# GateLoop and a SwiGLU block on one core: refitted schedule model, last output by halves, prefetch hints at the closing branch

## The chip, the cores and the metric

The kernel runs on one core of a Trainium2 chip. The engines are named as in the profile: PE is TensorE (matrix products; PEld its weight loads), DVE is VectorE, ACT is ScalarE, POOL is GpSimd, SP is SyncE, which here issues DMAs only. The metric is the time of one execution on the chip in microseconds (us): before, the median of three runs is 697.68 us (697.25 to 699.55). All numbers are float32.

## The reference

Four batches of eight heads with 768 positions of 48 features go through a linear attention with complex decay, the heads are laid side by side (384 features for each of 3072 tokens), and a SwiGLU block with RMS norm follows.

```python
mag = sqrt(a_re**2 + a_im**2);  scale = minimum(mag, 0.999) / (mag + 1e-6)
for t in range(S):                       # S = 768, per batch and head
    S_re, S_im = ar*S_re - ai*S_im + k[t] v[t]^T,  ar*S_im + ai*S_re     # 48 x 48
    y[t] = q[t] @ S_re
x = y, heads side by side                # 3072 x 384
xn = x / sqrt(mean(x*x) + 1e-6) * rms_g
out = (silu(xn @ w_gate) * (xn @ w_val)) @ w_out    # 384 -> 1536 -> 384
```

The three weight matrices arrive as float64.

## The kernel before

**Tiling.** Tokens are cut in 24 chunks of 128 (six for each batch). Gates are computed in units: chunks 0 and 1 are units of their own, the later units are pairs. Chunks also form twelve groups of two, and a group goes through the SwiGLU block together. Stages are named in the code: `load`, `kq`, `size`, `root`, `turn` and `rot` belong to the gates of a unit (magnitudes, rsqrt, angles by arctan and sin, q and k rotated by the accumulated decay), `attend`, `y`, `state` and `norm` to a chunk, `head` and `feed` to a group, `raw` and `w` to a piece of weights, `look` to a check of the weights' words.

**Gates and attention.** A unit's gates run mostly on ACT and DVE. ACT needs tables for sin, arctan, rsqrt and silu in turn, and each change is an ACT_TABLE_LOAD. The rotated q and k (`rot`, `kin`) are sent by six DMAs of SP into the tile kq, in the layout that attention needs: 96 rows (48 real and 48 imaginary) for each head. Chunks 0 to 3 alternate between kq0 and kq1; from chunk 4 on there is kq0 alone. On PE a chunk is scores (bank<-kq), masked by DVE (am<-causal,bank), then `y` (am,ve and kq,state), transposes of k (ident,kq) and the state's update (vn,kt). For the norm, ACT squares y, PE sums by a product with ones (ones,sq), ACT writes the sum to ssv, POOL raises it to the power -1/2 (rs<-ssv,mhalf), and the result is spread over the partitions: for chunks 4 to 21 by two DMAs, for the others by a PE product (ident,rs). DVE multiplies into xT.

**Weights.** Pieces of 128x3072 words come by POOL's DMA queue into space borrowed from wo and hT. ACT scales the low words (wo<-wo or hT<-hT, int32), and three DVE instructions (a shift, a bit operation and a custom addition) put the float32 weights into wg and wv. A piece's DMA waits for the piece two before it, by a small POOL copy (junk<-wo), and piece 4 for the copy seen<-kq1.

**Feed.** Group 0's first blocks (`head`) take one chunk at a time with 128-column products; the others have 256 columns. Groups from 2 on use sums of weight blocks to save products (`joint`), and `down` (L1418) gives the output product of a group from four blocks of 192 columns: x1 to x4 are PE's sums, and DVE combines them into ots[1] and ots[0]. `finish` (L1414) sends both, the last group's on ACT's DMA queue and the others on SP's.

**What sets the order.** Nothing is issued where it is written. `Flow.add` records an operation with its engine, an estimated duration and what it reads and writes; all have the helper's line 731. `dates` gives each operation a due date, backwards from the dates of the feed's products, and adds `flow.shift[(stage, i)]`. `schedule` then plays the engines forward with a model of their times: whenever an engine is free, it takes the waiting operation with the earliest due date among those that the model has ready (4.0 us are added where ACT's table would change). SP has eight lanes, so a ninth transfer waits for a landing. The order found so is what `issue` emits; each engine then works through its own queue in that order, and at run time waits for whatever is not ready.

**Fillers.** Up to WARM = 62 us of the model's time, where PE would wait, `schedule` puts in products into bank 3 of the first rotated tile with itself (bank3<-rot0). They compute nothing. They wait for the first rotated product (`started`) and keep PE busy; their number is fixed by the model, not at run time.

**End.** `fast` ends with a flag: a sum over checks of the gates and weights goes to bad. If it is above 0, `general` computes everything again in a way that has no such limits (L1675); with these inputs it is not.

Of the kernel before, what the change touches and what calls it, by code (L numbers as in the profile page):

```python
# [13 lines left out]
AF = mybir.ActivationFunctionType  # L14
ALU = mybir.AluOpType
# [4 lines left out]
C = 128  # L20
BLK = 32
# [479 lines left out]
class Flow:  # L501
# [10 lines left out]
    turn = 0.0  # L512
# [66 lines left out]
    def add(self, eng, calls, dur, reads=(), writes=(), table=None, land=None, due=None, after=(), behind=(), late=None, mode=None, group=None):  # L579
        over = self.OVERLAP.get(eng, 0.0) if land is None else 0.0  # L580
        shy = eng == "POOL" and land is None and calls[0][0] in (self.nc.gpsimd.tensor_tensor, self.nc.gpsimd.tensor_copy)
        grip = eng == "DVE" and bool(reads) and calls[0][0] != self.nc.vector.tensor_tensor_scan and not any(
            x.tensor.name in self.rooms and self.rooms[x.tensor.name][0].startswith("bank") for x in (*reads, *writes))
        op = dict(i=len(self.ops), eng=eng, calls=calls, dur=dur, deps=set(), table=table, land=land, over=over, grip=grip, shy=shy,
                  base=due, late=late, mode=mode, group=group, stage=self.stage, behind={o["i"] for o in behind})
# [30 lines left out]
    def schedule(self):  # L616
        users = self.dates()
        left = [len(op["deps"]) + len(op["behind"]) for op in self.ops]
        ready = [0.0] * len(self.ops)
        free = {}  # L620
# [12 lines left out]
        order = 0  # L633

# [8 lines left out]
        while True:  # L643
            best = None
            for eng, ops in waiting.items():
                if ops:
                    t = max(free[eng], min(ready[o["i"]] for o in ops))
                    if eng == "POOL":
                        t = min(max(free[eng], ready[o["i"]], held + 0.01 if o["shy"] else 0.0) for o in ops)
                    if eng == "SP" and len(sent) >= self.LANES:  # L650
                        if "landed" not in sent[-self.LANES]:
                            continue
                        t = max(t, sent[-self.LANES]["landed"])
                    if best is None or t < best[0]:
                        best = (t, eng)
            if queue:
                o = min(queue, key=lambda o: o["arrives"])
                t = max(served, o["arrives"])
                if best is None or t <= best[0]:
# [3 lines left out]
                    release(o, o["landed"])  # L663
                    continue
# [4 lines left out]
            for o in waiting[eng]:  # L669
                if ready[o["i"]] > t + 1e-9 or o["shy"] and t < held:  # L670
# [23 lines left out]
            if o["shy"] and t == held + 0.01:  # L694
                dur += 0.4
            if o["grip"]:
                held = t + dur
# [16 lines left out]
            order += 1  # L714
            free[eng] = t + dur - o["over"]
            release(o, t + dur, self.next)
# [17 lines left out]
def fast(tc, ctx, qT, kT, v, a_re, a_im, w_gate, w_val, w_out, rms_g, out, H, bad):  # L734
# [145 lines left out]
    def mm_time(n, m=P):  # L880
        return 2 * max(0.844e-3 * n, 0.872e-3 * m)
# [115 lines left out]
    def fetch(i, piece, raw, eng):  # L997
# [12 lines left out]
        pace = dict(load=1.9 + 1.0e-3 * raw.shape[1], lead=1.2) if eng == "POOL" else {}  # L1010
        sent = dma(raw3, src, eng, after=wait, **pace)
        if eng == "POOL":
            landed[i] = add("POOL", [(nc.gpsimd.tensor_copy, (), dict(out=junk, in_=raw[0:1, 1:2]))], 0.25,
                            after=[sent])
# [26 lines left out]
    def look(i):  # L1041
        flow.stage = "look", i
        to, ap, c, f = looks[i]
        if ap.dtype == FP32:
            for x in (small, large, whole):
                fill(x[:, i:i + 1], 0.0)
            return
        x = raws[i % len(raws)]
        lo, hi = fetch(i, looks[i], x, "SP")
        hf, lf = hi.bitcast(FP32), lo.bitcast(FP32)  # L1050
        act(hf, hf, AF.Abs, accum=whole[:, i:i + 1])
        act(lf, hf, AF.Relu, bias=most, accum=large[:, i:i + 1])
        act(lf, hf, AF.Relu, scale=-1.0, bias=least, accum=small[:, i:i + 1])
# [19 lines left out]
    def load_gates(u):  # L1073
# [15 lines left out]
        for name, ap in (("re", a_re), ("im", a_im)):  # L1089
            x = dma(t[name], ap[b].rearrange("(h j l) s -> l h j s", j=ND, l=L)[:, :, :, c * C:c * C + T],  # L1090
                    "ACT" if u < 2 and name == "im" else "SP", slow=0.75 if u > 1 else 0.0, behind=moved[HOLD] if u > 1 else (),
# [7 lines left out]
    def load_kq(u, t):  # L1099
        flow.stage = "kq", u  # L1100
        for name, ap in (("q", qT), ("k", kT)):
            for i, n in enumerate(UNITS[u]):
                dma(t[name][:, i],
                    ap[n].rearrange("d (h t) -> (d h) t", t=C).rearrange("(j p) t -> p j t", p=P),
                    behind=moved[HOLD] if u > 1 else rows_, group=("kq", u))
# [14 lines left out]
    def gates(u):  # L1120
# [85 lines left out]
        for i, n_ in enumerate(ns):  # L1206
# [4 lines left out]
            moved[n_] = [dma(kq[r:D2:2 * ND], x, "SP") for r, x in enumerate(rows[n_])]  # L1211
# [17 lines left out]
    def attend(n):  # L1229
# [5 lines left out]
        later = dict(behind=moved[min(n - 1, HOLD)] if n else (), group=("v", n))  # L1235
# [41 lines left out]
        mms(order, len(order) * mm_time(C) / 4 * 1.06, mode=BLK)  # L1277
# [36 lines left out]
        mms([(col, sq[:, j], ones, j == 0, j == parts[-1]) for j in parts], 0.25 * len(parts))  # L1314
# [103 lines left out]
    def down(ns, h, S1, S2):  # L1418
# [25 lines left out]
        tt(halves(ots[1]), halves(x1), mids[1][:, hi].unsqueeze(1).to_broadcast([C, 2, DH]), ALU.add)  # L1444
        product(x4[:, hi], S4, B[1, 1])
# [185 lines left out]
    for in_, limit, op in ((ef, P_MIN, ALU.is_ge), (ef, 1.0, ALU.is_le), (range_, 0.0, ALU.is_le),  # L1631
# [18 lines left out]
        ("attend", 11): 4.5, ("attend", 12): -1.5, ("attend", 16): 1.8, ("attend", 17): -13.3,  # L1650
        ("attend", 18): 4.0, ("attend", 19): 32.7, ("decay", 2): 6.2, ("feed", 0): 57.8, ("feed", 1): 13.4,
        ("feed", 4): 0.5, ("feed", 5): 2.1, ("feed", 6): -0.4, ("feed", 7): 57.5, ("feed", 9): 25.8,
        ("feed", 11): -11.2, ("form", 3): 17.6, ("kq", 3): -4.6, ("load", 0): 0.9, ("load", 1): -0.2,
        ("load", 2): -18.9, ("load", 3): 7.8, ("look", 10): -1.2, ("norm", 3): 0.1, ("norm", 14): 0.2,
        ("norm", 16): -2.1, ("norm", 19): 3.5, ("norm", 22): 9.5, ("raw", 0): -5.3, ("raw", 1): 3.2,
        ("root", 3): 0.2, ("root", 11): 0.2, ("rot", 2): -1.2, ("rot", 11): -19.8, ("size", 1): 1.3,
        ("size", 2): -19.9, ("size", 3): 47.2, ("size", 5): -12.4, ("size", 11): 63.2, ("state", 7): -18.0,
        ("state", 9): -18.1, ("state", 14): -10.5, ("state", 15): -17.9, ("state", 20): 19.7,
        ("state", 22): -19.0, ("turn", 1): -0.5, ("turn", 2): -0.2, ("turn", 4): -0.1, ("w", 0): 10.0,
        ("w", 1): 18.3, ("w", 2): -8.9, ("w", 3): -56.3, ("w", 5): 50.9, ("w", 7): 13.4, ("y", 6): -9.6,  # L1660
        ("y", 8): -0.5, ("y", 12): 11.1,
# [7 lines left out]
def gateloop_swiglu(tc, qT, kT, v, a_re, a_im, w_gate, w_val, w_out, rms_g, out, H):  # L1669
    nc = tc.nc  # L1670
    with tc.tile_pool(name="flag", bufs=1) as flag:
# [3 lines left out]
        with tc.If(nc.values_load(bad[0:1, 0:1]) > 0):  # L1675
            general(tc, qT, kT, v, a_re, a_im, w_gate, w_val, w_out, rms_g, out, H)

# [38 lines left out]
```

## Time and profile before

| | before |
|---|---|
| median of three runs | 697.68 us (697.25, 699.55, 697.68) |
| profiled execution | 700.69 us, 3.0 above the median |
| its span, first to last instruction | 699.0 us |
| mean granted PE clock | 0.989 |
| first product that the gates allow | 24.37 us |
| first feed product | 53.94 us |
| last product of PE | 692.09 us |
| activation table loads | 57 of 1283 ns |

The profile comes from one execution. Busy time counts instructions of an engine; the granted clock is what the throttle gave PE, 1.00 being full speed. In the timeline a row is a run of like instructions: its start, its length, engine, line, operation, output and inputs, tile shapes, and count; in brackets the engine's idle time ahead and the engine or DMA that ended it. SPq, ACTq and POOLq are the queues that issue DMAs.

### The profile page before, as it was taken

Reading aid. Unit: us, or ns where it says so; the run is one execution under the profiler, and the core shown is the slowest. Engines: PE = TensorE matmul, PEld = TensorE weight load, DVE = VectorE, ACT = ScalarE, POOL = GpSimd, SP = SyncE. Lnnn points to the kernel's source line nnn. Section 1 sums busy time; section 2 is a strip of 40 time slices with the busy share of each in tenths; the row PEclk is TensorE's granted clock in tenths of the full one; section 3 lists DMA queues with packets and bytes.
Section 4 is the critical chain, followed back from the end, with each engine's and each line's share of the span. In section 5 each row is a group of like instructions: output and inputs, shape, how many; then the busy total and the mean of one; then the engine's idle time right before and its main releaser. Section 6 shows DMA issues by size and latency. Waiting matters only on the chain.

```text
span 699.0 us, 19004 instructions
## 1 busy us (share of the span) xinstructions
PE 653.0 (93%) x7907; PEld 606.6 (87%) x7909; DVE 556.8 (80%) x1025; ACT 497.6 (71%) x864; POOL 78.9 (11%) x109
## 2 busy tenths in 40 slices
PE   0689998999999999999999999999999999999995
PEld 0679875886899999999999999999999898899995
DVE  8988979779999879879899879789889486256561
ACT  8667667896785775765878776686797765999750
POOL 3226022011013002001000002100000000000000
PEclk9979999999999999999999999999999999999999
DMA  9876671455514354253443434554140557654100
GB/s 286 284 220 205 184 214 23 114 116 121 125 28 72 80 110 75 75 111 56 112 82 70 120 71 96 139 118 110 55 88 14 135 165 186 210 187 152 54 1 28
DMA packets 104014, 82.01 MB, mean 117 GB/s; under 512 B 41936, under 2 KB 94416, under 8 KB 103920
## 3 DMA queue, kind: packets, MB, share of 16 engines
q1 hardware_dynamic: 98560, 64.78, 34.8%
q0 software_dynamic: 4416, 15.35, 10.5%
q8 instruction: 64, 1.05, 0.6%
q10 hardware_dynamic: 944, 0.59, 0.3%
q14 instruction: 30, 0.25, 0.1%
HBM read 55.84 MB, written 4.72 MB: 87 GB/s over the span
## 4 chain that ended last, share of the span: by engine, by line
PE 44%; issue 20%; DMA 10%; ACT 7%; DVE 3%; POOL 2%; SPq 1%; POOLq 0%; ACTq 0%; DVEq 0%
PE bank L731 44%; DMA sq<-rs 4%; ACT kin L731 2%; DMA hT<-in_w_out_dram 2%; POOL rs L731 2%; ACT rot L731 2%; DVE hT L731 1%; DMA row<-sq 1%; SPq L731 1%; DMA wo<-in_w_out_dram 1%; DMA rot<-in_w_val_dram 1%; ACT bank L731 1%; DMA kin<-in_w_val_dram 1%; DVE wo L731 1%; DMA kq<-kin 1%
## 5 line engine op out<-in xcount | busy, mean ns | idle before, releaser
L731 PE MATMUL bank<-wo,hT 128*128 128x192 f32 (+1 forms) x696 | 142.4, 353 | 0.6 <-DVE hT L731 0.4
L731 PEld LDWEIGHTS bank<-wo,hT 128*128 128x128 f32 x696 | 115.9, 191 | 12.2 <-issue 1.3
L731 PE MATMUL bank<-xT,wg 128*128 128x128 f32 (+1 forms) x488 | 84.8, 307 | 0.6 <-DVE wg L731 0.4
L731 ACT ACTIVATE hT<-bank 128x512 f32<-128x512 f32 x100 | 58.2, 593 | 37.7 <-PE bank L731 24.0
L731 PE MATMUL bank<-xT,wv 128*128 128x128 f32 (+1 forms) x488 | 83.5, 304 | 0.0
L731 POOL TENSOR_TENSOR rs<-ssv,mhalf 128x1 f32<-128x1 f32 x24 | 29.0, 1210 | 453.1 <-ACT ssv L731 380.4
L731 ACT ACT_TABLE_LOAD x57 | 73.1, 1283 | 7.7 <-DVE rot L731 3.9
L731 PEld LDWEIGHTS bank<-xT,wg 128*128 128x128 f32 x488 | 70.4, 191 | 6.6 <-issue 1.6
L731 PEld LDWEIGHTS bank<-xT,wv 128*128 128x128 f32 x488 | 70.9, 194 | 3.1 <-issue 0.2
L731 ACT ACTIVATE bank<-bank 128x512 f32<-128x512 f32 x60 | 35.1, 585 | 25.8 <-PE bank L731 21.2
L731 DVE TENSOR_TENSOR hT<-hT 128x768 f32<-128x768 f32 (+1 forms) x60 | 51.8, 863 | 0.4
L731 PE MATMUL bank<-yg,wg 128*128 128x128 f32 x320 | 50.6, 281 | 0.0
L731 PE MATMUL bank<-yg,wv 128*128 128x128 f32 x320 | 48.8, 275 | 0.0
L731 DVE TENSOR_TENSOR hT<-bank,hT 128x512 f32<-128x512 f32 x50 | 34.4, 688 | 15.4 <-PE bank L731 6.2
L731 DVE COPY_PREDICATED am<-causal,bank 128x512 f32<-128x512 int32 x48 | 35.0, 735 | 13.7 <-PE bank L731 13.7
L731 PE MATMUL bank<-sums,hT 128*128 128x192 f32 x240 | 45.0, 329 | 0.0
L731 PEld LDWEIGHTS bank<-yg,wg 128*128 128x128 f32 x320 | 42.1, 192 | 1.2 <-ACT sg L731 0.2
L731 ACT ACTIVATE sg<-bank 128x256 f32<-128x256 f32 (+1 forms) x72 | 38.1, 532 | 5.8 <-PE bank L731 3.9
L731 PEld LDWEIGHTS bank<-yg,wv 128*128 128x128 f32 x320 | 42.2, 192 | 0.0
L731 PE MATMUL bank<-am,ve 128*32 128x128 f32 x768 | 38.3, 281 | 1.6 <-DVE xT L731 1.4
L731 PEld LDWEIGHTS bank<-sums,hT 128*128 128x128 f32 x240 | 39.4, 190 | 0.3 <-DVE mid L731 0.2
L731 PEld LDWEIGHTS bank<-kq 96*32 96x32 f32 x1536 | 30.4, 110 | 9.8 <-issue 4.0
(217 smaller groups left out, 1449.3 us busy)
## 6 DMA issues: line engine op xcount, KB each, us to landing
kq<-rot SPq DMA_DIRECT2D x84, 128.0 KB, 2.4
kq<-kin SPq DMA_DIRECT2D x60, 128.0 KB, 2.5
kin<-in_q_dram SPq DMA_DIRECT2D x24, 192.0 KB, 3.1
kin<-in_k_dram SPq DMA_DIRECT2D x24, 192.0 KB, 3.9
out_dram<-ot SPq DMA_DIRECT2D x23, 192.0 KB, 2.5
in<-in_a_re_dram SPq DMA_DIRECT2D x11, 384.0 KB, 4.8
in<-in_a_im_dram SPq DMA_DIRECT2D x11, 384.0 KB, 4.4
vn<-in_v_dram SPq DMA_DIRECT2D x20, 192.0 KB, 2.8
```

The costliest lines, as they stand in the source:

```text
L731: fn(*args, **kw)
```

## The change

Three things change.

**The model.** `Flow.schedule` gets other durations: a PE product's end reaches other engines after 0.1 (0.055) us, a switch into the score products costs 0.225 (0.09), a table load 1.41 (1.3), PE products 0.849 and 0.877 ns an element and row (0.844, 0.872), and many DMAs get a later landing (`slow`). POOL's power is now an operation whose end is left open: if DVE works off the banks within 0.4 us of its start, it ends 0.43 us after DVE is through. A filler is counted at 0.26 us after the first ones (0.43), and fillers end when an operation writes bank 3. All dates in `flow.shift` are new. None of this is emitted: it decides only the order of the instructions and the number of fillers, which goes from 36 to 64.

**The last output.** For the last group ots[1] is sent on ACT; ots[0] is computed in halves of 192 columns, the low half earlier and sent on ACT, the high half last and sent on SP.

**The branch.** At the start PE, DVE, ACT and SP get a hint that names the closing branch, and the condition is turned round: if the flag is at most 0, the empty body is taken as the likely one; else `general` runs.

```diff
-        return 0.055 if x["eng"] == "PE" else 0.085 if x["eng"] == "POOL" else 0.034
+        return 0.1 if x["eng"] == "PE" else 0.085 if x["eng"] == "POOL" else 0.034
...
-            return 0.09
+            return 0.225 if o["stage"][0] == "attend" else 0.09
...
-        shy = eng == "POOL" and land is None and calls[0][0] in (self.nc.gpsimd.tensor_tensor, self.nc.gpsimd.tensor_copy)
+        shy = eng == "POOL" and land is None and calls[0][0] == self.nc.gpsimd.tensor_tensor
...
+            if power is not None:
+                t = held + 0.01 if shut else power["start"] + 0.4
+                if best is None or t <= best[0]:
+                    power["end"] = held + 0.43 if shut else power["start"] + power["dur"]
+                    free["POOL"] = power["end"]
...
-                dur += 1.3
+                dur += 1.41
...
-            if eng == "PE" and self.warm and t < self.warm["until"] and all("end" in x for x in self.warm["after"]):
+            if eng == "PE" and self.warm and not claimed and t < self.warm["until"] and all("end" in x for x in self.warm["after"]):
                 since = max([free["PE"]] + [x["end"] + 0.06 for x in self.warm["after"] if not recent])
-                n = int((t - since - 0.3) / 0.43)
+                step = 0.26 if recent else 0.43
+                n = int((t - since - 0.25) / step)
                 if n > 0:
                     self.fillers.append((order - 0.5, n))
-                    recent.append((since, since + 0.43 * n))
+                    recent.append((since, since + step * n))
+            claimed = claimed or o["claims"]
...
-            moved[n_] = [dma(kq[r:D2:2 * ND], x, "SP") for r, x in enumerate(rows[n_])]
+            moved[n_] = [dma(kq[r:D2:2 * ND], x, "SP", slow=0.3) for r, x in enumerate(rows[n_])]
...
+        if ns[-1] == N - 1:
+            dma(out[ns[1] * C:(ns[1] + 1) * C, :], ots[1], "ACT")
+            tt(ots[0][:, lo], mids[0][:, lo], x4[:, lo], ALU.add)
+            dma(out[ns[0] * C:(ns[0] + 1) * C, lo], ots[0][:, lo], "ACT")
+            product(x4[:, hi], S4, B[1, 1])
+            tt(ots[0][:, hi], mids[0][:, hi], x4[:, hi], ALU.add)
+            dma(out[ns[0] * C:(ns[0] + 1) * C, hi], ots[0][:, hi], "SP")
+            return
...
-        ("attend", 11): 4.5, ("attend", 12): -1.5, ("attend", 16): 1.8, ("attend", 17): -13.3,
+        ("attend", 6): -2.0, ("attend", 10): 27.7, ("attend", 13): -59.0, ("attend", 15): -9.6,
...
+    tc.mark_branch_hint_location("passed", engines=[mybir.EngineType.PE, mybir.EngineType.DVE,
+                                                    mybir.EngineType.Activation, mybir.EngineType.SP])
...
-        with tc.If(nc.values_load(bad[0:1, 0:1]) > 0):
+        with tc.If(nc.values_load(bad[0:1, 0:1]) <= 0, label="passed", preferred_fallthrough_block=False) as passed:
+            pass
+        with passed.Else():
             general(tc, qT, kT, v, a_re, a_im, w_gate, w_val, w_out, rms_g, out, H)
```

What the order becomes is shown at three places. A row has the line, the operation, output and inputs by name (the number behind a name's underscore counts tiles), the shape, and how often it repeats.

**First place, the start.** PE's first instructions before: three small products for the decays, 29 fillers, the other three small products, and the scores of chunk 0.

```order
L731 MATMUL bank0_65<-ot1_135,ot0_134 96x8 x3
L731 MATMUL bank3_68<-rot0_106 128x128 x29
L731 MATMUL bank1_66<-ot1_135,ot0_134 96x8 x3
L731 MATMUL bank4_69<-kq0_108 32x128
L731 MATMUL bank4_69<-kq0_108 32x96
L731 MATMUL bank4_69<-kq0_108 32x64
L731 MATMUL bank4_69<-kq0_108 32x32
```
PE's first instructions after the change:

```order
L1749 BRANCH_PREFETCH_HINT
L746 MATMUL bank0_69<-ot1_139,ot0_138 96x8 x3
L746 MATMUL bank1_70<-ot1_139,ot0_138 96x8 x3
L746 MATMUL bank3_72<-rot0_110 128x128 x54
L746 MATMUL bank4_73<-kq0_112 32x128
L746 MATMUL bank4_73<-kq0_112 32x96
L746 MATMUL bank4_73<-kq0_112 32x64
L746 MATMUL bank4_73<-kq0_112 32x32
```
The small products stand together ahead of the fillers, of which there are 54 in place of 29, all ahead of the scores. ACT in the gates of the first two units (in0<-in0,mid and in0,width check that the inputs lie in range, t1 and t2 are the magnitudes, in0<-in0 is the arctan, once for each unit), around the load of arctan's table, before:

```order
L731 ACTIVATE in0_99<-in0_99,mid_79 128x384
L731 ACTIVATE t2_103<-t4_104 128x384
L731 ACTIVATE t1_102<-t2_103 128x384
L731 ACTIVATE t2_103<-t4_104 128x384
L731 ACTIVATE t1_102<-t2_103 128x384
L731 ACT_TABLE_LOAD
L731 ACTIVATE in0_99<-in0_99 128x384 x2
L731 ACTIVATE in0_99,range__85<-in0_99,width_80 128x384
```
ACT at the same place after:

```order
L746 ACTIVATE t2_107<-t2_107,ones_80 128x384
L746 ACTIVATE in0_103<-in0_103,mid_83 128x384
L746 ACTIVATE in0_103,range__89<-in0_103,width_84 128x384 x2
L746 ACTIVATE t2_107<-t4_108 128x384
L746 ACTIVATE t1_106<-t2_107 128x384
L746 ACT_TABLE_LOAD
L746 ACTIVATE in0_103<-in0_103 128x384 x2
```
One mid operation and both width operations, which stood behind the load and the arctans, now stand ahead of them.

**Second place, between chunk 0's scores and the first feed products.** POOL before: copies that see a landing (seen, junk), the weight pieces' DMAs and the powers of chunks 0 and 1.

```order
L731 COPY junk_139<-hT_95 1x1 x2
L731 COPY seen_140<-kq0_108 96x1
L731 COPY seen_140<-kq1_109 96x1
L731 DMA wo_94<-in_w_val_dram 128x3x1024
L731 TENSOR_TENSOR rs0_129<-ssv_128,mhalf_75 128x1
L731 COPY junk_139<-wo_94 1x1
L731 TENSOR_TENSOR rs1_130<-ssv_128,mhalf_75 128x1
L731 DMA hT_95<-in_w_out_dram 128x2x768
```
POOL after:

```order
L746 COPY junk_143<-hT_99 1x1 x2
L746 COPY seen_144<-kq0_112 96x1
L746 TENSOR_TENSOR rs0_133<-ssv_132,mhalf_79 128x1
L746 COPY seen_144<-kq1_113 96x1
L746 DMA wo_98<-in_w_gate_dram 128x3x1024
L746 TENSOR_TENSOR rs1_134<-ssv_132,mhalf_79 128x1
L746 DMA wo_98<-in_w_val_dram 128x3x1024
L746 COPY junk_143<-wo_98 1x1 x2
```
The power of chunk 0 now stands ahead of the copy seen<-kq1 and with it ahead of the next weight piece, and the gate piece comes before the value piece. DVE's queue from chunk 0's masks (am0) on, after the change (ISA is the custom addition):

```order
L746 COPY_PREDICATED am0_120<-causal_78,bank4_73 128x512
L746 COPY_PREDICATED am0_120<-causal_78,bank5_74 128x512
L746 TENSOR_SCALAR wv_97<-wo_98 128x1536
L746 ISA wg_96<-hT_99,wg_96 128x3072
L746 TENSOR_TENSOR state0_127<-bank5_74,decay0_114 96x8x48
L746 SCALAR_TENSOR_TENSOR wv_97<-hT_99,wv_97 128x1536
L746 COPY_PREDICATED am1_121<-causal_78,bank4_73 128x512
L746 COPY_PREDICATED am1_121<-causal_78,bank5_74 128x512
L746 TENSOR_TENSOR xT0_100<-yg0_130,bank7_76 128x3x128
L746 SCALAR_TENSOR_TENSOR wv_97<-wo_98,wv_97 128x1536
L746 ISA wv_97<-hT_99,wv_97 128x3072
L746 ISA wv_97<-wo_98,wv_97 128x3072
```
The two masks of chunk 0 come behind earlier weight work; between them and the last additions for wv lie the rows shown.

**Third place, the norm of chunk 3.** ACT before (kt is the transposed k, sq and yg belong to the norm, hT<-hT scales a weight piece, the table loads are rsqrt's and arctan's of a later unit):

```order
L731 ACTIVATE kt0_118<-bank7_72 128x384
L731 ACTIVATE hT_95<-hT_95 128x768
L731 ACTIVATE sq0_125<-bank6_71 128x384
L731 ACT_TABLE_LOAD
L731 ACTIVATE t2_103<-t4_104 128x768
L731 ACTIVATE yg1_127<-bank6_71,gcol_82 128x128
L731 ACT_TABLE_LOAD
L731 ACTIVATE in0_99<-in0_99 128x768
L731 ACTIVATE ssv_128<-bank7_72,floor_78 128x1
```
ACT after:

```order
L746 ACTIVATE kt0_122<-bank4_73 128x384
L746 ACTIVATE sq0_129<-bank6_75 128x384
L746 ACTIVATE yg1_131<-bank6_75,gcol_86 128x128
L746 ACTIVATE hT_99<-hT_99 128x768
L746 ACTIVATE ssv_132<-bank7_76,floor_82 128x1
L746 ACTIVATE yg1_131<-bank6_75,gcol_86 128x128 x2
L746 ACTIVATE wo_98<-wo_98 128x768
L746 ACTIVATE t2_107<-t4_108 128x768
L746 ACT_TABLE_LOAD
```
The sum ssv of chunk 3 moved from behind the two table loads and the arctan's operations to ahead of them.

More of the change, by code (lines that the diff above doesn't have):

```diff
@@ L658, in schedule @@
                 t = max(served, o["arrives"])
-                if best is None or t <= best[0]:
+                if (best is None or t <= best[0]) and (power is None or t <= (held + 0.01 if shut else power["start"] + 0.4)):
                     queue.remove(o)
@@ L663, in schedule @@
                     release(o, o["landed"])
+                    continue
+            if power is not None:
[3 more added lines that the diff above has]
+                    free["POOL"] = power["end"]
+                    release(power, power["end"], self.next)
+                    release(power, power["end"])
+                    power = None
                     continue
@@ L714, in schedule @@
             order += 1
+            if o["grip"]:
+                if power is not None and t < power["start"] + 0.4:
+                    shut = True
+                held = t + dur
             free[eng] = t + dur - o["over"]
+            if o["shy"]:
+                power, shut, free[eng] = o, t < held, 1e6
+                continue
             release(o, t + dur, self.next)
@@ L1050, in look @@
         hf, lf = hi.bitcast(FP32), lo.bitcast(FP32)
-        act(hf, hf, AF.Abs, accum=whole[:, i:i + 1])
-        act(lf, hf, AF.Relu, bias=most, accum=large[:, i:i + 1])
-        act(lf, hf, AF.Relu, scale=-1.0, bias=least, accum=small[:, i:i + 1])
+        looked = []
+        looked.append(act(hf, hf, AF.Abs, accum=whole[:, i:i + 1]))
+        looked.append(act(lf, hf, AF.Relu, bias=most, accum=large[:, i:i + 1]))
+        looked.append(act(lf, hf, AF.Relu, scale=-1.0, bias=least, accum=small[:, i:i + 1]))
+        for o in looked:
+            o["dur"] += 0.07
     EARLY = {0: -100.0, 1: -98.0}
@@ L1090, in load_gates @@
             x = dma(t[name], ap[b].rearrange("(h j l) s -> l h j s", j=ND, l=L)[:, :, :, c * C:c * C + T],
-                    "ACT" if u < 2 and name == "im" else "SP", slow=0.75 if u > 1 else 0.0, behind=moved[HOLD] if u > 1 else (),
+                    "ACT" if u < 2 and name == "im" else "SP", slow=0.75 if u < 2 else 2.5, behind=moved[HOLD] if u > 1 else (),
                     due=u - 310.0 if u < 2 else None)
@@ L1234, in attend @@
         vv = vns[0]
-        later = dict(behind=moved[min(n - 1, HOLD)] if n else (), group=("v", n))
+        later = dict(slow=1.5 if n > 1 else 0.4, behind=moved[min(n - 1, HOLD)] if n else (), group=("v", n))
         rows = v[n * C:(n + 1) * C, :].rearrange("t (m e d) -> t m e d", e=2, d=D)
@@ L1655, in fast @@
[L1655 to L1659, printed above, removed]
```

48 lines of the change are left out of this document (28 added, 20 removed).

## Prediction

> **What bounds the kernel now.** The page comes first, its span and busy times.
>
> ```profile
> span 699.0 us, 19004 instructions
> PE 653.0 (93%) x7907; PEld 606.6 (87%) x7909; DVE 556.8 (80%) x1025; ACT 497.6 (71%) x864; POOL 78.9 (11%) x109
> ```
>
> TensorE (PE) is busy 93% of the span; the next engine, DVE, 80%. PE's products stay the same but for fillers, so the change can only win or lose time in which PE stands still, runs fillers or runs at half clock. The windows by stage say where that is.
>
> ```profile
> 34.20:54.00 19.80, 17.19 (x368) 14.89 (x367) 17.73 (x24) 13.63 (x24) 5.25 (x6) 0.78 0.73 205
> 54.00:120.00 66.00, 61.25 (x627) 49.91 (x626) 58.28 (x79) 43.79 (x61) 20.74 (x15) 0.96 0.58 163
> 120.00:692.00 572.00, 564.22 (x6848) 531.78 (x6848) 449.76 (x864) 414.45 (x740) 42.44 (x56) 1.00 0.42 99
> ```
>
> Columns of the windows: stretch and length, busy time of PE, its weight loads, DVE, ACT and POOL, granted clock, DMA share, GB/s. Four stages follow from it: the front to 54 us, where PE waits for the first gates and the narrowed weights; 54 to 120, with 4.75 us idle and a clock of 0.96; 120 to 692, with 7.8 us idle in 572; and the tail of 6.9 us after PE's last product at 692.09.
>
> **The front.** The timeline, with start, duration, engine, operation and, in brackets, the wait ahead:
>
> ```profile
> 13.66 1.28 ACT L731 ACT_TABLE_LOAD   x1
> 15.80 0.60 ACT L731 ACTIVATE in<-in,width 128x384 f32<-128x384 f32 x1
> 23.36 0.96 DVE L731 TENSOR_TENSOR rot<-kin,turns 128x768 f32<-128x768 f32 x1
> 24.37 8.57 PE L731 MATMUL bank<-rot 128*128 128x128 f32 x58 [3.78 <-DVE rot L731]
> 24.00:28.00 4.00, 3.63 (x17) 3.63 (x18) 3.96 (x6) 3.18 (x6) 0.35 (x1) 1.00 0.97 313
> 28.00:32.00 4.00, 4.00 (x37) 4.00 (x37) 4.00 (x5) 2.07 (x2) 0.19 (x1) 1.00 0.80 194
> 32.19 1.31 POOL L731 COPY seen<-kq 96x1 f32<-96x1 f32 x1 [2.89 <-DMA kq<-rot]
> 34.21 1.33 PE L731 MATMUL bank<-kq 96*32 96x128 f32 x64
> 53.94 3.69 PE L731 MATMUL bank<-xT,wv 128*128 128x128 f32 x24
> 57.47 2.84 PE L731 MATMUL bank<-xT,wg 128*128 128x128 f32 x24
> ```
>
> First, ACT's load of arctan's table moves behind three more operations (a mid and both width operations, in the order of ACT above). At up to 0.60 us each the first rotated product is between nothing (where ACT waits anyway) and 1.8 later, taken as 1.6, hence ready at 24.32 + 1.6 = 25.9. Then the fillers: the order puts 54 of them ahead of chunk 0's scores instead of 29. Each makes two passes (29 gave 58 records). The first 17 took 3.63 / 17 = 0.214 us, the later ones 4.00 / 37 = 0.108 us, so 108 passes take 3.63 + 91 x 0.108 = 13.5 us, up to 14.6 at the rate of the whole row (8.57 us for 58). They end at about 39.5 to 40.5, and chunk 0's scores start at **39.8 instead of 34.21**, though POOL's copy saw their kq landed at 32.19. The model now counts 0.26 us a filler, the rows say 0.216 warm and 0.43 cold; its end of the train is therefore nearly right if it starts when the model has it, and late by as much as the first rotated product is late. As PE takes its queue in order, a train that runs over holds the scores, and this is 5.6 us of delay there. The model's other constants emit nothing; they and the table of dates act through the order alone.
>
> Not all of it reaches the first feed products (the heads, 53.94). Between scores and heads lie 19.7 us, of which 19.8 - 17.2 = 2.6 are PE waits and 0.22 x 19.8 = 4.4 are lost clock. Meanwhile DVE goes on narrowing weights.
>
> ```profile
> 36.52 0.95 DVE L731 TENSOR_SCALAR wv<-hT 128x1536 int32<-128x1536 int32 x1
> 37.39 1.74 DVE L731 CUSTOM_DVE_ANT_0 wv<-wo,wv 128x3072 uint16<-128x3072 uint16 x1
> 39.53 1.74 DVE L731 SCALAR_TENSOR_TENSOR wv<-hT,wv 128x1536 int32<-128x1536 int32 x1
> 43.48 0.73 DVE L731 COPY_PREDICATED am<-causal,bank 128x512 f32<-128x512 int32 x1
> 52.62 0.55 DVE L731 TENSOR_TENSOR xT<-yg,bank 128x384 f32<-128x384 f32 x1 [1.19 <-PE bank L731]
> 41.53 2.47 POOL L731 TENSOR_TENSOR rs<-ssv,mhalf 128x1 f32<-128x1 f32 x1 [1.06 <-ACT ssv L731]
> 51.93 0.65 PE L731 MATMUL bank<-ident,rs 128*128 128x128 f32 x2 [0.43 <-POOL rs L731]
> 39.61 0.77 PE L731 MATMUL bank<-kq 96*32 96x128 f32 x32 [1.31 <-DMA in<-in_a_im_dram]
> 42.00:44.00 2.00, 1.56 (x8) 1.26 (x7) 2.00 (x2) 1.97 (x3) 2.00 (x1) 0.50 1.02 356
> ```
>
> By the new order DVE's queue behind chunk 0's masks holds, up to the heads, a shift 0.95, three custom additions 5.22, two bit operations 3.48, a state 0.55, two masks 1.46 and one xT 0.55, together 12.2 us, beside it POOL's power (2.47) and its broadcast (0.65): 15.3 us as the least, 19.7 as the most. I take 0.9 over the least, 16.2: heads at 39.8 + 16.2 = **56.0, 2.1 later**. They then run behind a busy PE, 2.84 instead of 3.69: -0.85. The half clock at 42.00 (0.50) came 2.4 us after a wait of 1.31 us, so small waits can bring it to the heads again; that 0.85 is in the range. *The Trainium skill, "TensorE: Matmul & The Clock Gate", Part 1, says that the clock falls only after a whole idle window of about 3.4 us; the row at 42.00 speaks against it. By that rule the heads could not be cold after the change.*
>
> Power 0 now stands ahead of the next weight piece on POOL:
>
> ```profile
> 39.69 0.78 POOL L731 DMA_DIRECT2D wo<-in_w_val_dram  x1 [4.29 <-DVE state L731]
> wo<-in_w_gate_dram POOLq DMA_DIRECT2D x2, 1536.0 KB, 10.5
> ```
>
> The DMA went out at 39.69; now it waits for the power, at 41.53 + 5.6 + 2.47 = 49.6 with the delay, and lands 10.5 later, at about 60. Its scaling on ACT stands ahead of the silu that frees PE's bank; between nothing and 2.9 us of wait (the lateness of the first rotated product and a table load), taken as 0.8. Front: 2.05 - 0.85 + 0.8 = **+2.0**.
>
> **54 to 120.**
>
> ```profile
> 107.97 2.83 PE L731 MATMUL bank<-wo,hT 128*128 128x384 f32 x8
> 109.69 0.24 ACT L731 ACTIVATE ssv<-bank,floor 128x1 f32<-128x1 f32 x1
> 113.91 0.79 PE L731 MATMUL bank<-ident,rs 128*128 128x128 f32 x2 [3.12 <-POOL rs L731]
> 114.50 3.98 PE L731 MATMUL bank<-wo,hT 128*128 128x384 f32 x8
> ```
>
> Chunk 3's sum of squares (ssv) waited behind two table loads on ACT, POOL's power after it, and PE 3.12 us for the power; right behind it the same 8 products took 3.98 instead of 2.83. In the new order ssv stands ahead of table load and arctan. The stage lost 4.75 us idle, 3.12 of them here, and 1.15 of clock: 5.9. I put it at 1.7 after, the 1.63 of short waits that nothing in the order removes: **-4.2**. Nothing else is late behind it: the gates that ACT pushes back have their chunk a full feed later.
>
> **120 to 692.**
>
> ```profile
> 24.34 4.05 SPq L731 DMA_DIRECT2D kq<-rot  x6
> 555.46 0.55 PE L731 MATMUL bank<-ident,kq 96*128 96x96 f32 x4 [1.37 <-DMA kq<-kin]
> kq<-kin SPq DMA_DIRECT2D x60, 128.0 KB, 2.5
> ```
>
> One buffer kq serves all chunks, so PE's last read of chunk n and first read of n+1 have to lie apart by six sends on SP's queue (4.05) and a landing (2.5): 6.55 us. Counting PE's work between them in both orders, at the spacings of the trace, eight changes of chunk had 6.5 to 7.2 us before (the 1.37 us at 555.46 is one that came too late) and three have 6.5 to 6.9 after, at chunks 8, 16 and 18. The cover of the other transfers is PE's work on the feeds, which now lies between. The stage's idle time is 572 - 564.22 = 7.8; between nothing and 6 of it can go (the rest are waits too short to see), and I take a little over the middle, since more than half of the tight changes are gone: **-3.3**.
>
> **The tail.**
>
> ```profile
> 692.13 0.55 DVE L731 TENSOR_TENSOR ot<-mid,bank 128x384 f32<-128x384 f32 x1 [0.42 <-PE bank L731]
> 692.71 0.36 ACTq L731 DMA_DIRECT2D out_dram<-ot  x1
> out_dram<-ot ACTq DMA_DIRECT2D x1, 192.0 KB, 4.2
> out_dram<-ot SPq DMA_DIRECT2D x1, 192.0 KB, 1.8
> SPq L1675 <- SPq L1675: 4.1, 2, 2.5
> 687.78 0.35 DVE L731 TENSOR_TENSOR mid<-mid,bank 128x192 f32<-128x192 f32 x1
> ```
>
> The last addition is half as wide: 0.35 for 0.55. The send of 192 KB on ACT landed after 4.2 us while SP's took 1.8, and the span ends 2.1 us behind that landing (692.71 + 4.2 to 699.0). The last half goes on SP: at 1.8, 0.2 + 2.4 = **-2.6**, if SP doesn't wait for the code behind the branch. Before it did: 2.5 us on SP at line 1675. Should the hint do nothing, SP comes past the branch 0.6 + 2.5 us after PE's end and has 2.9 us of closing waits left: 6.2 for 6.9, -0.7. *The Trainium skill, "Runtime: NRT & Kernel Launch", Instruction fetch mechanics, has prefetch as purely sequential and a taken branch as a forced fetch; SP's 2.5 us agree, and by it the hint would leave that wait: the rival below.* The 28 fillers more are in the front; the hint itself is one row on four engines, beside the waits of the first 24 us, at nothing.
>
> **Sum:** +2.0 - 4.2 - 3.3 - 2.6 = -8.1 against the profiled execution, 700.7 to 692.6. It is 3.0 above the median of 697.68. PE's idle from its first filler on is 22 us (2.6 + 4.75 + 7.8 + 6.9); the terms that remove waits make 10.1 of it, so of an excess spread over the waits 1.4 lie in them. For the median I count -6.7: **691.0**.
>
> **Rivals.** *A, the front is earlier:* DVE is ahead with the weights and heads come at 53, at full clock, with no wait for the piece: 691.0 - 3.0 - 0.8 = 687.2. For it: DVE has 5.6 us more before the scores. Against: its queue behind the masks. *B, the hint does nothing:* 691.0 + 1.9 = 692.9; for it SP's 2.5 us. *C, the fillers cost one for one:* heads at 53.94 + 5.6 = 59.5, and 1.2 more for the piece: 691.0 + 3.5 + 1.2 = 695.7. For it: the 19.7 us between scores and heads stay a chain of DVE, POOL and PE; against: the 2.6 us of waits and 4.4 us of clock in it. *D, slower:* the delay of C moves all later gates, sends and dates away from where the new table had them, so that 120 to 692 wins nothing and 54 to 120 only the power's 3.12: 695.7 + 3.3 + 1.1 and, with B, 1.9 give 702. It decides from heads 8.7 us late (4.2 + 3.3 + 2.6 - 1.4) if the rest comes as forecast, and from some 4 us (3.12 + 0.7, and little of the excess) if the middle wins nothing and the hint is idle. Nothing in the rows shows the later waits come back; but the waits there were of one execution.
>
> **How the numbers follow.** Forecast 691.0 with 0.47 (its own range 688.5 to 693.5), A 0.13, B 0.15, C 0.12, D 0.13. The range reaches A's better end (687.2 less a full 2.0 in the middle) and C's worse one, 685.5 to 697. 0.3%, about what a measurement of this kernel can tell from no change, is 695.6 to 699.8: C lies on the lower edge, half of it counts as same, and a quarter of D. Faster 0.80, same 0.10, slower 0.10.
>
> **What would show it.** Filler train of 108 passes ending near 39.8, heads at 56 (right) or 59.5 (C); chunk 3's power no longer waited for; fewer waits <- kq after 120; the last send on SP landing in 1.8 and no 2.5 us at the branch (B if it stays). Wrong if DVE's narrowing lies ahead of the heads alone, or if PE's waits past 120 exceed 7.8 us.

## The result, and the profile after

| | before | after |
|---|---|---|
| median | 697.46 us (694.34 to 699.55, 6 runs) | 690.94 us (688.12 to 691.84, 6 runs) |
| profiled execution, span | 700.69, 699.0 | 691.83, 690.1 |
| granted clock, mean | 0.989 | 0.996 |
| scores of chunk 0 | 34.21 | 39.94 |
| first feed products | 53.94 | 56.17 |
| first product of the weight sums (group 2) | 220.33 | 216.27 |
| PE's last product | 692.09 | 685.72 |
| from there to the span's end | 6.9 | 4.4 |

The ratio after to before is 0.990, with a 95% interval of 0.987 to 0.993. Forecast were 691.0 for the median and 692.6 for the profiled execution. The profile of before is of an execution longer than any of its six, 3.2 us above their median. Of the six after, the two whose mean granted clock was 1.000 took 688.12 and 688.35 us, the four at 0.995 to 0.997 took 690.59 to 691.84. The front of the changed kernel in the timeline:

```profile
25.70 14.31 PE L746 MATMUL bank<-rot 128*128 128x128 f32 x108 [6.37 <-DVE rot L746]
31.61 0.49 POOL L746 COPY seen<-kq 96x1 f32<-96x1 f32 x1 [2.92 <-DMA kq<-rot]
39.94 1.33 PE L746 MATMUL bank<-kq 96*32 96x128 f32 x64
56.17 2.84 PE L746 MATMUL bank<-xT,wg 128*128 128x128 f32 x24
100.74 0.27 ACT L746 ACTIVATE ssv<-bank,floor 128x1 f32<-128x1 f32 x1
103.22 0.38 PE L746 MATMUL bank<-ident,rs 128*128 128x128 f32 x2
```

The filler train starts 1.3 us later than before and holds the scores until 39.94, eight microseconds after their kq was seen to have landed at 31.61. The feed follows 2.2 us later than before, at full clock. Chunk 3's power is no longer waited for: its row (103.22) has no bracket, where 3.12 us stood.

From the first feed products to the first product of the weight sums, and from there to PE's last product, PE has the same work in both kernels. The windows of before:

```profile
53.94:220.33 166.39, 161.60 (x1752) 134.99 (x1751) 149.00 (x233) 120.14 (x185) 30.77 (x25) 0.98 0.49 125
220.33:692.09 471.76, 464.02 (x5724) 446.75 (x5723) 359.10 (x710) 338.15 (x616) 32.41 (x47) 1.00 0.41 99
```

and of the changed kernel:

```profile
56.17:216.27 160.10, 158.85 (x1752) 133.77 (x1751) 151.95 (x240) 119.69 (x185) 20.18 (x27) 1.00 0.49 127
216.27:685.72 469.45, 463.76 (x5725) 447.23 (x5723) 359.43 (x713) 346.02 (x620) 28.35 (x45) 1.00 0.41 100
```

1752 PE records in both: 166.39 us became 160.10. Idle time fell from 4.79 to 1.25, and busy time by 2.75, as the clock went from 0.98 to 1.00. In the long middle, idle time fell from 7.74 to 5.69. With the later start and the tail, 2.2 - 6.3 - 2.3 - 2.5 = -8.9, the difference of the spans.

The two largest waits left past 120 us are these rows of the timeline:

```profile
464.24 0.52 PE L746 MATMUL bank<-ident,kq 96*128 96x96 f32 x4 [2.14 <-issue]
572.22 0.99 PE L746 MATMUL bank<-kq 96*32 96x128 f32 x32 [1.93 <-DMA decay<-ends]
```

The first is chunk 18's. SP sent three pieces of v first, so its kq set out at 454.89, 2.2 us after PE's last read of chunk 17, and the last two sends took 4.6 us to land. The second is chunk 22's scores; its kq, sent behind a piece of raw weights, took 5.2 and 5.7 us to land (three DMAs each), not the 2.5 and 2.6 of the whole kernel's medians:

```profile
in<-in_w_val_dram SPq DMA_DIRECT2D x1, 768.0 KB
kq<-rot SPq DMA_DIRECT2D x3, 128.0 KB, 5.2
kq<-kin SPq DMA_DIRECT2D x3, 128.0 KB, 5.7
```

The profile names the DMAs of decay as what ended this wait. The scores read kq alone, its last send landed at about the same moment, and five of the seven other runs of this order have the same wait with kq<-kin as its end.

The tail, in the DMA view (KB each, us to landing) and in SP's waits (in total, times, longest; line 1709 is the branch):

```profile
out_dram<-ot ACTq DMA_DIRECT2D x1, 192.0 KB, 2.5
out_dram<-ot SPq DMA_DIRECT2D x1, 96.0 KB, 2.0
```

```profile
SPq L1709 <- SPq L1709: 0.7, 2, 0.5
```

SP's wait of 2.5 us at the branch is gone. So is the slow landing on ACT's queue: 2.5 us for 192 KB, where 192 KB had taken 4.2. It isn't the same send, though. The 4.2 us were the last output's; the 192 KB on ACT are now the output before it, which went on SP before.

### The profile page after: what moved, and what is told of

Read it like the earlier page. It is cut to its first block, busy times and chain, and to the rows that moved or that the text cites. A ratio compares the mean times of both kernels' runs of the same rounds, so it can differ in the third digit from the quotient of the medians.

```text
span 690.1 us, 19118 instructions
## 1 busy us (share of the span) xinstructions
PE 652.9 (95%) x7965; PEld 609.6 (88%) x7965; DVE 556.2 (81%) x1026; ACT 499.6 (72%) x864; POOL 63.7 (9%) x109
## 3 DMA queue, kind: packets, MB, share of 16 engines
q0 software_dynamic: 4416, 15.35, 10.5%
## 4 chain that ended last, share of the span: by engine, by line
PE 76%; DVE 8%; issue 4%; SPq 4%; DMA 4%; ACT 3%; POOL 0%; DVEq 0%; POOLq 0%; ACTq 0%
PE bank L746 76%; SPq L746 4%; DVE turns L746 1%; DVE hT L746 1%; DVE t L746 1%; DMA decay<-ends 1%; ACT in L746 1%; ACT t L746 1%; DMA in<-in_w_val_dram 1%; DMA ve<-in_v_dram 1%; DVE rot L746 1%; DVE am L746 1%; ACT L746 1%; DMA vn<-in_v_dram 1%; ACT bank L746 1%
## 5 line engine op out<-in xcount | busy, mean ns | idle before, releaser
L746 PE MATMUL bank<-wo,hT 128*128 128x192 f32 (+1 forms) x696 | 140.7, 350 | 0.0
L746 POOL TENSOR_TENSOR rs<-ssv,mhalf 128x1 f32<-128x1 f32 x24 | 21.4, 890 | 461.5 <-ACT ssv L746 407.9
L746 ACT ACTIVATE bank<-bank 128x512 f32<-128x512 f32 x60 | 35.2, 586 | 17.9 <-PE bank L746 11.4
L746 PE MATMUL bank<-kq 96*32 96x128 f32 (+3 forms) x1536 | 36.4, 237 | 3.1 <-DMA decay<-ends 1.9
```

Of the source, the lines that this page charges most:

```text
L746: fn(*args, **kw)
```

## The experiments

Each was timed in several rounds beside the kernel before on the same chip. The ratios are to that kernel; 0.001 is 0.7 us. They ran in three groups of four, each group on another chip (before: medians of 698.1, 696.75 and 696.8 us), so across groups only the ratios compare. Within a group a difference is given by the medians and, where it matters, by the ratios too.

**The changed kernel again**, as the measure for the next three.

> The changed kernel unaltered, as the measure for the three kernels beside it. Theory (the sum of the prediction): 6 to 9 us under the kernel before. Scores of chunk 0 at 39.9, first feed products at 56.2, PE's last product 4.4 us before the span's end. Whether the half clock that the profiled execution showed at 572.62 (after a wait of 1.93 us) comes back: if it belongs to that one wait, an execution without such a wait has clock 1.00 and is about 1.7 us shorter.

690.27 us (688.82 to 691.67, 6 runs), before on this chip 698.1, ratio 0.989 (0.987 to 0.991). Its front, and a tail of 4.2 us:

```profile
41.20 1.33 PE L746 MATMUL bank<-kq 96*32 96x128 f32 x64
58.46 3.33 PE L746 MATMUL bank<-xT,wg 128*128 128x128 f32 x24
```

PE waited 2.09 us at 571.04, with no half clock after it: such a wait doesn't always bring it. In this execution the clock halved at 56.06, within a wait of 1.71 for a power.

**Without the hints.**

```diff
-    tc.mark_branch_hint_location("passed", engines=[...])
```

> The changed kernel without the prefetch hints on the four engines; the condition stays turned round. Theory H (the hints fetch the code behind the branch): SP waits 2.5 us at the closing branch again, so the tail from PE's last product to the span's end grows from 4.4 to about 6.2 us, and the time by 1.8. Rival (a taken branch fetches its target whatever was hinted, or turning the condition alone did it): no wait returns, the time stays within 0.5 us of the changed kernel.

692.48 us (691.73 to 695.08), ratio 0.994 (0.992 to 0.996), 2.2 us over the run above (3.2 by the ratios). PE's last product is at 683.72 and the span 690.2: a tail of 6.5 instead of 4.2 us. SP's waits:

```profile
SPq L1707 <- SPq L1707: 2.8, 1, 2.8
```

Theory H holds; turning the condition alone does nothing for the wait. The two last sends, 96 KB on ACT's queue and 96 KB on SP's, landed in 1.7 us each here.

**Without the halves.**

```diff
-        if ns[-1] == N - 1:
-            ...
-            return
```

> The changed kernel with its last output as before: one addition of 384 columns and one send of 192 KB on ACT's queue. Theory T1 (the prediction's: the send on ACT is slow in landing, 4.2 us against 1.8): +0.2 for the addition and +2.2 for the landing, 2.4 us longer. Rival T2 (the landing of 4.2 us was long because code was being fetched at that moment, which the hints have moved away): landing at about 2.5, +0.2 and +0.5, 0.7 us longer.

693.35 us (690.53 to 694.72), ratio 0.993 (0.991 to 0.995). In the profile the tail is 5.0 us (PE's end 688.01, span 693.0), 0.8 more. The landings in it:

```profile
out_dram<-ot SPq DMA_DIRECT2D x1, 192.0 KB, 1.9
out_dram<-ot ACTq DMA_DIRECT2D x1, 192.0 KB, 2.3
```

The tail is T2's: 2.3 us on ACT's queue with the hints, 4.2 without. The time is 3.1 us over the changed kernel run again (2.7 by the ratios), more than the tail explains. PE came to the feed at 58.37, as in that run, but it ran at half clock for longer, from 55.7 to 62.57 and again from 574.57, which the edit doesn't touch.

**29 fillers instead of 54**, the order otherwise the same.

```diff
+        self.fillers[0] = (self.fillers[0][0], 29)
         steps += [(at, self.warm["call"] * n) for at, n in self.fillers]
```

> The changed kernel with 29 instead of 54 fillers in the first train; the order is otherwise the same, instruction by instruction. Theory F (the train runs over by about 6 us and the scores wait for it): scores of chunk 0 at 32.5 to 33.5 instead of 39.94, chunk 1's at about 40.5 when its kq has landed, instead of 45.14; first feed products 3 to 5 us earlier, at 51 to 53; the time 2.5 to 4.5 us less. Rival C (without the train the clock falls, and the waits for gates and weights come instead): PE waits 34 to 40 us with nothing to do, granted clock 0.5 in part of 40 to 56, first feed products at 55 to 56.5; the time within 1 us of the changed kernel, or more.

**684.37 us** (684.1 to 690.13), ratio 0.984 (0.981 to 0.987), under the changed kernel on this chip by 5.9 us (3.8 by the ratios; two of the six runs took 687.8 and 690.13). Its timeline:

```profile
25.36 8.73 PE L747 MATMUL bank<-rot 128*128 128x128 f32 x58 [6.37 <-DVE rot L747]
34.02 1.33 PE L747 MATMUL bank<-kq 96*32 96x128 f32 x64
53.62 2.84 PE L747 MATMUL bank<-xT,wg 128*128 128x128 f32 x24
```

and its window from 28 to 54 us, with the granted clock third from the end:

```profile
28.00:54.00 26.00, 23.16 (x424) 21.69 (x423) 21.73 (x24) 11.47 (x22) 5.48 (x8) 0.87 0.88 229
```

Scores came 7.2 us earlier than in the changed kernel run again, the feed 4.8 earlier, though the clock was 0.87 between 28 and 54 us. Both theories have a part: the train did run over, and with the short one the clock does fall. By the ratio this run is 11.4 us under before. The tail makes up to 2.7 of that in the profiles (6.9 to 4.2), so some 9 us are left for the order.

**The tail alone on the kernel before**: halves, hints, turned condition.

> The kernel before with the tail's part of the change alone: last output by halves, hints, condition turned round; order and dates of before. The two runs without hints and without halves gave 2.3 and 0.8 us in the tail (6.5 and 5.0 us from PE's last product to the span's end, for 4.2). Theory: the tail falls from 6.9 to 4.2 to 4.4 us and the time by 2.5 us against before, with PE's last product where it was. Rival (code fetched earlier delays transfers elsewhere): less than 1.5.

696.52 us (693.09 to 698.07, 12 runs) beside 696.75 (23 runs), ratio 0.999 (0.997 to 1.001). In the profile the tail is what was expected (PE's end 687.21, span 691.4: 4.2), but the median shows at most 2.2 us of it. In this execution, the shortest of the twelve, the feed began at 51.67, with order and fillers of before, where the first profile had 53.94:

```profile
51.67 4.44 PE L731 MATMUL bank<-xT,wv 128*128 128x128 f32 x24
```

The front alone differs by two microseconds between executions.

**54 fillers in the kernel before**, its order kept (the same edit, with 54).

> The kernel before with 54 instead of 29 fillers in its first train, the order otherwise unchanged. Theory F1 (25 fillers cost what they cost in the changed kernel, one for one): scores of chunk 0 at about 40 instead of 34.2, first feed products 4 to 6 us later, the time 4 to 6 us longer. Theory F2 (the prediction's: DVE narrows weights meanwhile, so that 2.1 of 5.6 us reach the feed): first feed products at 56, half clock gone from 42 to 49, the time 1 to 2 us longer.

701.04 us (697.16 to 702.87, 12 runs), ratio 1.005 (1.002 to 1.007): 3.2 us longer by the ratio, 1.7 to 4.7.

The timeline of its front:

```profile
24.39 14.99 PE L732 MATMUL bank<-rot 128*128 128x128 f32 x108 [3.78 <-DVE rot L732]
39.74 1.33 PE L732 MATMUL bank<-kq 96*32 96x128 f32 x64
56.12 2.94 PE L732 MATMUL bank<-xT,wv 128*128 128x128 f32 x24
```

The feed at 56.1 is F2's number; against 51.67 above it is F1's 4.5. The time lies between the two. The half clock that F2 wanted gone is not: the granted clock is 0.93 between 28 and 54 us.

**The new model with the old dates.** `flow.shift` of before in the changed kernel.

> The changed kernel, with its refitted model, its tail and its hints, but the table of dates of the kernel before; the model then puts 45 fillers in the first train. Theory M (the refitted model makes the better order by itself, the dates matter little): within 1.5 us of the changed kernel, 690. Theory D (the dates are tuned to their model and carry the order): the gain in the order is lost, the tail's 2.6 stay: 695 or more; ssv of chunk 3 or other sums of squares wait behind table loads again, PE waits for powers or for kq.

709.75 us (708.82 to 714.61), ratio 1.019 (1.016 to 1.023). PE's waits from 54 us on:

```profile
PE bank L746 <- ACT bank L746: 3.2, 4, 2.2
PE bank L746 <- DVE hT L746: 3.1, 5, 1.2
PE bank L746 <- ACT ot L746: 2.8, 1, 2.8
PE bank L746 <- DVE xT L746: 2.7, 1, 2.7
```

**The old model with the new dates.** The table alone in the kernel before.

> The kernel before, with its model, its tail and without hints, but the new table of dates; its model puts 33 fillers in the first train. Theory D: no better than before (698 or more on this chip), since these dates were set against other durations. Theory M2 (the dates are a better order whatever the model): 692 to 694, that is the changed kernel less the tail's 2.6.

716.19 us (712.31 to 722.55), ratio 1.027 (1.023 to 1.032). Its waits stand elsewhere:

```profile
PE bank L731 <- ACT bank L731: 4.9, 9, 1.2
PE bank L731 <- ACT sg L731: 3.3, 3, 2.6
PE bank L731 <- DMA vn<-in_v_dram: 3.2, 1, 3.2
PE bank L731 <- DMA kq<-kin: 3.1, 2, 2.0
```

Either half of the refit alone is 13 to 19 us slower than before. Theory D holds, and by more than it said: dates and durations are one thing. The number of fillers changed too (81 and 47, for 64 in the changed kernel), but the feed starts at 57.40 and 57.83 us, within the changed kernel's 56.17 to 58.46; the loss lies behind the front, in many waits.

**14, 22 and 40 fillers** in the changed kernel (the same edit).

> The changed kernel with 14 fillers in its first train (28 passes, 17 x 0.214 + 11 x 0.108 = 4.8 us: ends at about 30.4, before chunk 0's kq has landed at about 32). Theory F (only the overrun past the landing costs): scores at 32.0 to 32.5, about 2 us earlier than with 29, the time 0 to 2 us under that run's 684.4. Rival C (the clock needs the train up to the scores): PE idle for 1.5 us ahead of the scores and a window at half clock between 32 and 50 that 29 fillers do not have there; first feed products no earlier, the time 684 to 687.

> The changed kernel with 22 fillers (44 passes, 3.63 + 27 x 0.108 = 6.5 us: ends at about 32, when kq lands). Theory F: scores at 32.2 to 32.7, 1.5 us earlier than with 29; the time 683 to 684.5. Rival C: as with 14, but without the idle time, so clock as with 29 and time as there, 684.4.

> The changed kernel with 40 fillers (80 passes, 10.4 us: ends at about 36). Theory F, one for one: scores at 36.3, 2.3 us later than with 29 and 3.6 earlier than with 54, the time on the line between 684.4 and 690.3: 686.5 to 687. Rival S (a step, because a fixed event decides, such as the fetch of PE's instructions or the clock's window): 684 to 685, or 689 to 691.

| fillers | median us | ratio (interval) | scores | first feed products | clock, 28 to 54 us |
|---|---|---|---|---|---|
| 14 | 685.65 | 0.983 (0.979 to 0.986) | 31.99 | 53.31 | 0.87 |
| 22 | 685.58 | 0.985 (0.981 to 0.990) | 32.47 | 52.47 | 0.87 |
| 29 | 684.37 | 0.984 (0.981 to 0.987) | 34.02 | 53.62 | 0.87 |
| 40 | 684.93 | 0.984 (0.980 to 0.987) | 36.22 | 51.54 | 1.00 |
| 54 | 690.27 | 0.989 (0.987 to 0.991) | 41.20 | 58.46 | 1.00 |

The rows of 29 and 54 are of another chip than the rest; their ratios compare with the others'. The line that F drew from 29 to 54 isn't there, and neither is the gain below 29. With 40 the scores are later, but the clock is full, as its timeline and window show:

```profile
25.74 10.55 PE L747 MATMUL bank<-rot 128*128 128x128 f32 x80 [6.38 <-DVE rot L747]
51.54 3.02 PE L747 MATMUL bank<-xT,wg 128*128 128x128 f32 x24
```

```profile
28.00:54.00 26.00, 24.46 (x465) 22.75 (x464) 23.04 (x25) 12.75 (x23) 5.47 (x7) 1.00 0.86 228
```

The clock of whole executions says the same of every run: 0.998 to 1.000 in the five with 40 fillers, 0.991 to 0.997 in those with 14 and 22, 0.993 to 0.999 with 29. So up to 40, a later start of the scores goes with a fuller clock, and the time stays. Past 40 there is little clock left to win, and 14 fillers more move the feed from 51.54 to between 56.17 and 58.46. So S is nearest, with the clock as the step. That the clock is what makes up for the lateness is argued from these figures; no run held it fixed.

**The tail on the kernel before, without PE's hint.**

> The kernel before with the tail's part of the change, the hint left out on PE only, so that PE's instructions stand where they stood; VectorE, ScalarE and SyncE keep it. With the hint on PE too the profile's tail was 4.2 us instead of 6.9, but the median only 0.2 us under before. Theory P (the row ahead of PE's stream moves its blocks of code and costs what the tail wins): tail 4.2 and the time 2 to 2.7 us under before. Rival N (it's spread by chance, in the front, of one or two us between executions): within 1 us of the run with the hint on PE; tail 4.2.

695.18 us (691.05 to 697.74, 12 runs) beside 696.8, ratio 0.996 (0.994 to 0.999), a tail of 4.2. By the ratio that is 2.6 us under before, 1.0 to 4.4, and theory P's number; but its interval overlaps that of the run with PE's hint (0.997 to 1.001). Whether the row ahead of PE's stream costs anything stays open.

## Why the prediction was right

**The front's dates.** The first rotated product came at 25.7 (25.9 in the prediction), the train's 108 passes took 14.3 us (13.5 to 14.6), the scores came at 39.94 (39.8) and the feed at 56.17 (56.0), at 2.84 us for 24 products. The wait of 0.8 for the weight piece didn't come. It went out at 47.33, not 49.6, landed 8.3 us later, not 10.5, and was in time.

**The front's price was mis-sized**, in the step "heads at 39.8 + 16.2 = 56.0, 2.1 later". 56.0 was right in the profiled execution; in three others of the changed front the feed came at 56.29, 58.37 and 58.46. And 53.94 as the measure was not right: it is the latest of three profiled executions of the old order and fillers (51.67 and 52.95 are the others). On average the scores came 6.3 us later and the feed 4.5. What the overrun costs is read from runs: 3.2 us for 25 fillers in the old order, 3.8 by the ratios and 5.9 by the medians in the new one (29 against 54). The prediction had DVE's narrowing hide most of it, 2.1 of 5.6 being left; the front is nearer to rival C, one for one. That C's total, 695.7, didn't come is because the order won more than was counted.

**54 to 120** was right in mechanism: chunk 3's ssv ahead of the table loads, no wait for the power, clock 1.00, and 1.1 us of idle time between the feed's start and 120 for 1.7 forecast. The wait for that power, 3.1 us, stands in all four profiled executions of the old order and in none of the eight of the new one. From the feed's start to 216 us the kernel won 6.3 us, where -0.85 + 0.8 - 4.2 = -4.25 was forecast. Of the difference, 0.8 is the stall that didn't come, 0.75 is clock (busy time fell by 2.75, for 0.85 + 1.15 counted) and the rest is idle time.

**120 to 692** was mis-sized and partly misplaced. Idle time fell by 2.05 past the weight sums, not by 3.3. The three changes of chunk named as tight, out of chunks 8, 16 and 18, did have 6.6, 7.2 and 6.9 us between PE's reads, and waits of nothing, 0.55 and 0.25; in the seven other executions of this order the last of them waited 0.8 to 1.8. The two large waits, into chunks 18 and 22, weren't named: their reads lie 11.55 and 9.34 us apart, but the count took the sends to start at once and to land in 2.5 us everywhere. Here SP was 2.2 us late with the first, and the landings took 4.6 us and, behind a weight piece on the same queue, 5.7.

**The tail's sum** was right (-2.5 for -2.6), its step "the last half goes on SP: at 1.8, 0.2 + 2.4" was not. The tail is 6.9 us with neither hints nor halves, 6.5 with halves alone, 5.0 with hints alone, 4.4 and 4.2 with both: the hints carry most of it, and the halves add 0.8 once the hints are there. The last send of 192 KB on ACT landed in 2.3 us with hints and 4.2 without, so the queue alone wasn't the reason. That code being fetched stood in its way is one reading. It is not shown: without hints the last 96 KB on SP landed in 1.7 us while SP waited 2.8 at the branch.

**Rival B** (the hints do nothing, 0.15) is refuted: without them SP waits 2.8 us. Its tail was 6.5 us, for 6.2 in the prediction, whose own terms, 0.6 + 2.5 + 2.9, make 6.0. By the Trainium skill, "Runtime: NRT & Kernel Launch", Instruction fetch mechanics, prefetch is purely sequential, and a taken branch to code outside the two pages that the engine holds forces a fetch. The 2.8 us without hints agree, the 0.5 with them doesn't. **A** didn't come as no feed product was early, and **D** neither: idle time past the weight sums fell, and chunk 3's wait went.

That the median came within 0.1 us of the forecast is in part luck: the front's cost and the order's gain up to 216 us were both too small in the sum, the gain after it too large, and they cancelled.

**Faster than both** is the changed kernel with its train cut to 29 or 40 fillers: 684.37 and 684.93 us, 0.984 of before each. The first, timed beside the changed kernel, is under it by 3.8 us by the ratios and 5.9 by the medians.

## What to carry to other kernels

Work put in to keep an engine warm should not run far past the landing of what the engine waits for; here 14 to 40 fillers took the same time, later scores going with a fuller clock, and 14 more cost some 4 to 5 us. A table of dates tuned on a model is part of that model: change both and tune again, or neither. And before a term of a sum is taken as the difference to a profiled moment, see how far that moment wanders between executions.

## What the runs showed of the hardware

The granted clock went to 0.5 after waits shorter than the time that it then stayed there: from 572.62 to 576.04, 3.4 us, after a wait of 1.93. In the changed kernel's timeline, four products ahead of the wait at 570.29 and four behind it, and two windows, with the granted clock third from the end:

```profile
569.68 0.61 PE L746 MATMUL bank<-yg,wv 128*128 128x128 f32 x4
575.01 1.06 PE L746 MATMUL bank<-xT,wg 128*128 128x128 f32 x4
570.29:572.22 1.93, 0.01 (x1) 0.04 (x2) 0.69 (x1) 1.57 (x3) 0.00 (x0) 1.00 0.30 24
574.00:575.00 1.00, 1.00 (x6) 1.00 (x6) 0.93 (x3) 0.00 (x0) 0.00 (x0) 0.50 1.62 68
```

0.61 us became 1.06. After 2.09 us at the same place in the second execution of this kernel the clock stayed full. The Trainium skill, "TensorE: Matmul & The Clock Gate", Part 1, wants at least one whole idle window of about 3.4 us for the fall; the rows disagree.

In the front PE also waits for what the profile calls issue, between like products that depend on nothing new. The changed kernel, and the one with 29 fillers:

```profile
54.51 0.28 PE L746 MATMUL bank<-vn,kt 128*32 128x48 f32 x5 [1.19 <-issue]
```

```profile
45.70 0.30 PE L747 MATMUL bank<-kq,state 96*32 96x128 f32 x2 [2.04 <-issue]
```

In the second execution of the changed kernel the same 48 products (vn,kt) ran without a gap, in 0.88 us. What PE waits for there wasn't tried apart.
